# Linear attention and a leaky-ReLU layer pair on one core: tile 6's second layer as seven block products, the last batch's attention earlier

## The chip, the core and the metric

One core of a Trainium2 chip runs the whole kernel in one launch. The metric is device time in microseconds (us), lower is better. Beside the time of a run stands the span of a profiled execution: from its first to its last instruction.

## What is computed

Eight batches, eight heads, 576 rows and 64 columns a head give 4608 tokens of 512 features. `q` is made a softmax over its columns, `k` a softmax over the rows; the attention is linear (no product of q with k). Its output goes through two layers:

```python
kv = np.einsum('bhsd,bhse->bhde', k_s, v)            # per head 64 x 64
x  = np.einsum('bhsd,bhde->bhse', q_s, kv)           # then (4608, 512)
h  = x @ w_in                                        # (4608, 2048)
g  = np.maximum(0.01 * h, h)
out = g @ w_out                                      # (4608, 512)
```

## The kernel before, in words

The 4608 tokens are nine tiles of 512 (tiles 0 to 8). TensorE does all products: the attention of each batch, then for each tile the first layer (16 blocks of hidden features, line 563) and the second (line 584, 64 matmuls of 512 columns for a tile). The attention is spread over the tiles: softmax of batch b + 1, its `kv` and the attention of batch b run while tile t's layers are on TensorE. The order on every engine is written out by hand. `at(t, u, ...)` (line 595) puts functions at a place: in tile t, u from 0 to 15 is behind that block of the first layer, u from 16 to 31 is behind a quarter of a 128-token part of the second layer. All engines take their instructions in this program order, and each waits in its own queue for what it reads; VectorE (DVE), ScalarE (ACT) and GpSimd (POOL) do the elementwise work, SyncE (SP) issues most DMAs, among them a transposing DMA per batch (`q_turn`, line 548) which brings the softmax of q into the layout that the attention reads.

The hand-written places that the change touches (lines 740 to 776): `k_front` takes the maximum of k over rows (`k_tree`, `k_allmax`) and subtracts it, `q_front` does the same for q, `q_exp` and `k_exp` are ACT's exponentials, `q_back` sums, normalizes and issues the transposing DMA, `casts` turns v to bf16 on POOL, `attend_kv(b)` does the attention of batch b mixed with the `kv` product of batch b + 1. The last batch, 7, has its attention behind tile 6's first layer (line 850).

Tiles 7 and 8 are computed differently, since both come last and all their operands are in SBUF. Their two layers use a 2 x 2 block scheme in which seven products take the place of eight (Strassen's, in Winograd's form). For the first layer the blocks are the two tiles' tokens (`XA`, `XB`) against the two halves of features and hidden units: for each of the eight pairs of hidden blocks, `pair_layer1(i, fills)` (line 1046, called a round here, i = 0 to 7) makes seven products of two matmuls. Some of the operands are sums of blocks: `s1` to `s4` of tokens (`token_sums`, line 832), `t1` to `t4` of weights (`in_weight_sums`, line 812, POOL), copied to a type that fp32r matmuls take. In a round, `px` is one PSUM bank to which four products are added one after the other, and it is copied out between them (`e1`, `u2`, `u3`): `pair_first` makes the first one, `t2`·`s2`, `t3`·`s3` and `t4`·`a22` follow, each of them waiting for the copy before it. `pw` (`pair_second`) and `py` (`t1`·`s1`, and later `b22`·`s4` in `pair_third`) are banks of their own. The results are summed on DVE (line 1018), go through `leaky` (line 572, ACT's Prelu) and are kept in bf16 as rows `g7` and `g8`.

While a round waits for its copies, TensorE is given other work, the *fill*: the second layer of tile 6. `fill_steps` yields after each matmul, and `between(n)` takes n of them; the tuple in line 1101 says how many go into which of a round's three places. The first quarter of tile 6's second layer, with the first products of round 0, runs ahead of the rounds (line 1097).

For the second layer of tiles 7 and 8 (from line 1107) each tile is its own 2 x 2 scheme: tokens and hidden units are halved, and the output columns `E1`, `E2`. The weights' sums `v1` to `v4` and a copy `o22` are made once (`out_weight_sums`, line 804); the row sums `r1` to `r4` and the copy `c22` for each tile. Each product is 16 matmuls of 256 columns (line 1118). Tile 7's `r1` and `r3` begin on POOL during the rounds (`sums_ahead`, line 999).

Of the kernel before, what the change touches and what calls it, by code (L numbers as in the profile page):

```python
# [20 lines left out]
L = 64  # L21
# [5 lines left out]
def kernel(  # L27
# [736 lines left out]
    at(2, 27, lambda: attend_kv(3))  # L764
    for t in range(3, B - 1):
        b, last = t + 1, t + 2 == B
        q_front(b, t - 1, 19 if last else 29)
        at(t - last, 24 if last else 2, lambda b=b: q_exp(b, ALLR))
        if not last:
            k_front(b + 1, t, 1, 8)  # L770
            casts(b + 1, t, 6)
            at(t, 17, lambda b=b: k_exp(b + 1, ALLH))
            at(t, 23, lambda b=b: attend_kv(b))
        q_back(b, t - last, 25 if last else 5)
        if b + 2 < B:
            at(t, 5, lambda b=b: load_all(b + 2))

# [25 lines left out]

    def out_weight_sums():
        w = lambda fh, os: w_out_sb[:, fh * NH : (fh + 1) * NH, os]
        subtract(nc.vector, "v1", w(0, E2), w(0, E1))
        subtract(nc.vector, "v2", w(1, E2), plain("v1"))
        subtract(nc.vector, "v3", w(1, E2), w(0, E2))
        subtract(nc.vector, "v4", w(1, E1), plain("v2"))
        nc.gpsimd.tensor_copy(out=late["o22"], in_=w(1, E2))  # L810

    def in_weight_sums(i):
        w = lambda cs, fh: w_in_sb[:, cs, (fh * NH + i) * P : (fh * NH + i + 1) * P]
        for n, k in zip(("t1", "t2", "t3", "t4"), range(4)):
            late[n, i] = late["t"][:, k, i % 2 * 256 : i % 2 * 256 + 256].rearrange("p (c f) -> p c f", c=2)
        for n, x, y in (
            ("t1", w(CL, 1), w(CL, 0)),
            ("t2", w(CR, 1), plain(("t1", i))),
            ("t3", w(CR, 1), w(CL, 1)),
            ("t4", w(CR, 0), plain(("t2", i))),  # L820
        ):
            subtract(nc.gpsimd, (n, i), x, y)
        if i > 1:
            last_weights(i)

    def last_weights(i):
        late["b22", i] = late["pool"].tile([P, 2, P], F32R, name="b22")
        nc.gpsimd.tensor_copy(out=late["b22", i], in_=w_in_sb[:, CR, (NH + i) * P : (NH + i + 1) * P])

    pairs = ctx.enter_context(ExitStack())  # L830

    def token_sums():
# [10 lines left out]
        subtract(nc.vector, "s4", xT[:, CR, XA], plain("s2"))  # L843
        last_weights(0)
        last_weights(1)
# [93 lines left out]
    def layer2_at(t, g, tsub, pool=psO_pool, tag="pout"):  # L939
        po = pool.tile([P, O], FP32, name="pout", tag=tag)  # L940
        for j in range(NF):
# [5 lines left out]
            yield  # L947

    for t in range(1, TA):
        g_sb = []  # L950
        for j in range(NF):
            ph = psB_pool.tile([P, TT], FP32, name="ph", tag=BANK_TAG)
            layer1(j, ph, t * TT, TT)
            if j % 2 == 0:
                g_sb.append(g_pool.tile([P, 2, TT], BF16, name="gj"))
            leaky(g_sb[j // 2][:, j % 2], ph)
# [41 lines left out]

    def sums_ahead(n, names=("r1", "r3")):
        if n == 0:  # L1000
            for name in ("r3", "r1"):
                late_rows(name, name, late["ahead"])
        (ms, h0), (_, h1) = g7_blocks(0)[n], g7_blocks(1)[n]
        ops = dict(r1=(h1(0), h1(1), ALU.add), r3=(h0(0), h1(0), ALU.subtract))
        for name in names:
            x, y, op = ops[name]
            eng = nc.vector if n == 3 else nc.gpsimd
            eng.tensor_tensor(out=late[name][:, ms], in0=x, in1=y, op=op)

    def bank():  # L1010
        return psB_pool.tile([P, TT], FP32, name="pp", tag=BANK_TAG)

    def product(ps, w, a, first=True):
        for c in range(2):
            nc.tensor.matmul(ps, lhsT=w(c), rhs=a(c), start=(first and c == 0), stop=(c == 1), skip_group_check=True)  # L1015

    def add(o, ps, e):
        nc.vector.tensor_tensor(out=o, in0=ps, in1=e, op=ALU.add)  # L1018

    of = lambda n: (lambda c: late[n][:, c])  # L1020
    keep = lambda n: late["pool"].tile([P, TT], FP32, name=n)
    firsts, thirds = {}, {}

    def pair_first(i):
        ps, e1 = bank(), keep("e1")
        product(ps, lambda c: w_in_sb[:, c, i * P : (i + 1) * P], lambda c: xT[:, c, XA])
        nc.scalar.copy(out=e1, in_=ps)
        firsts[i] = ps, e1

# [4 lines left out]

    def pair_c11(i, ps):
        e1 = firsts[i][1]
        add(e1, ps, e1)
        leaky(g7[i], e1)

    def pair_third(i):  # L1040
        py, u2 = thirds[i]
        product(py, of(("b22", i)), of("s4"), False)
        add(u2, py, u2)
        leaky(g7[NH + i], u2)

    def pair_layer1(i, fills):
        px = firsts[i][0]
        u2, u3 = keep("u2"), keep("u3")
        g7_rows(i)
        if i == 0:  # L1050
            pw = pair_second(i)
            between(2)
        product(px, of(("t2", i)), of("s2"), False)
        if i:
            nc.vector.tensor_copy(out=u2, in_=px)
            pw = pair_second(i)
        else:
            nc.scalar.copy(out=u2, in_=px)
        if i + 1 < NH:
            pair_first(i + 1)  # L1060
        if i:
            pair_c11(i, pw)
            pair_third(i - 1)
        between(fills[0])
        product(px, of(("t3", i)), of("s3"), False)
        if i:
            nc.vector.tensor_copy(out=u3, in_=px)
        else:
            nc.scalar.copy(out=u3, in_=px)
            pair_c11(i, pw)  # L1070
        py = bank()
# [3 lines left out]
        add(u3, py, u3)  # L1075
        leaky(g8(NH + i), u3)
        if i == 0:
            nc.gpsimd.tensor_copy(out=gate, in_=u3[:, 0:1])
# [3 lines left out]
        if i + 2 < NH:  # L1082
            in_weight_sums(i + 2)
        if i in (2, 4, 6):
            sums_ahead(i // 2 - 1)

    def fill_steps():
        for tsub in range(1, NTS):
            yield from layer2_at(TA - 1, g_sb, tsub)

# [12 lines left out]
    next(fill, None)  # L1103
    pairs.close()
# [22 lines left out]
    def row_sums(wide, name, n, pool, op, x, y, eng=nc.vector):  # L1127
        late_rows(name, n, pool)
        for (ms, h0), (_, h1) in zip(wide(0), wide(1)):
            view = lambda s: late[s][:, ms].bitcast(FP32) if isinstance(s, str) else (h0, h1)[s[0]](s[1])  # L1130
            o = late[name][:, ms]
            if op is None:
# [11 lines left out]
    B8 = dict(t=TB, g=g8, wide=g8_wide, each=True, issue=(nc.sync, nc.scalar), r1="r1b", r2="r2b")  # L1144

    def put(z, o, half, i, cols, issues=None):
        for n, issue in enumerate(issues or z["issue"]):
            b, c = divmod(z["t"] * TT + half * M2 + i * P + n * L, S)
            issue.dma_start(out=out_r[b, c // L, :, cols], in_=o[n * L : (n + 1) * L, cols])

# [29 lines left out]
    def seventh(z):  # L1180
        product2(z["x"], rows("r3"), rows("v3"), z["each"], first=False)
        snap(z, "u3")

    def fourth(z):
        product2(z["x"], rows("c22"), rows("v4"), z["each"], first=False)
        for i in range(2):
            nc.scalar.copy(out=z["o2"][i][:, E1], in_=z["x"][i])
            put(z, z["o2"][i], 1, i, slice(0, O))

# [3 lines left out]
    def c11(z):  # L1193
        for i in range(2):
            add(z["o1"][i][:, E1], z["w"][i], z["e1"][:, i])
            put(z, z["o1"][i], 0, i, E1, (nc.sync, nc.sync))

# [4 lines left out]
    def c12(z):  # L1202
        for i in range(2):
            add(z["o1"][i][:, E2], z["y"][i], z["u2"][:, i])
            put(z, z["o1"][i], 0, i, E2)

    def sums(z, n):
        pool = late["ahead"] if n == "r3" else last_pool
        name = "r2b" if z is B8 and n == "r2" else n
        row_sums(z["wide"], name, name, pool, *dict(  # L1210
            r2=(ALU.subtract, z["r1"], (0, 0)),
# [11 lines left out]
    first(A)  # L1223
    sums_ahead(3, ("r1",))
    sums(A, "r2")
# [4 lines left out]
    c11(A)  # L1230
    sums_ahead(3, ("r3",))
    second(B8)
# [5 lines left out]
    seventh(A)  # L1238
    A["o2"], B8["o2"] = out_pairs(), [last_pool.tile([P, O], FP32, name=f"o{i}") for i in range(2)]
    sixth(B8)  # L1240
# [44 lines left out]
```

## Time and profile before

| | |
|---|---|
| median of 3 runs | 278.25 us (278.16 to 278.36) |
| the profiled execution | 278.23 us, of which the span is 276.4 us |
| instructions in the span | 5216, of these 2018 matmuls |
| TensorE clock granted | 1.00 throughout |
| HBM | 36.70 MB read, 9.44 MB written, 167 GB/s over the span |

All times within the execution are us from the span's start. A row of the chain or of a timeline begins with start and duration; matmuls overlap each other, so the pace is taken from start to start. A row of a group gives count, busy time and mean duration in ns of one, then the idle time of the engine before them and what ended it. PEld is TensorE's loading of weights. In the table of stages each engine has its busy us in the stretch and its count of instructions, then come the granted clock, the DMA share and GB/s.

### The profile page before, as it was taken

What the parts mean: (1) busy time and instruction counts of PE and PEld (TensorE: products, weight loads), DVE (VectorE), ACT (ScalarE), POOL (GpSimd) and SP (SyncE); (2) the same over time, 40 slices, a digit from 0 to 9 for tenths busy, and PEclk for the clock granted to TensorE, in tenths of its full rate; (3) what the DMA queues carried; (4) which work ended last, traced back from release to release, by engine and by line L of the source; (5) the groups of instructions that cost most, each with busy time, mean ns of one, the idle gap of its engine ahead of it and who ended that gap; (6) DMA issues with size and microseconds to landing.
All of it is one profiled execution on the core that took longest, in us unless ns stands there. A gap on an engine that the chain in (4) does not pass through costs nothing.

```text
span 276.4 us, 5216 instructions
## 1 busy us (share of the span) xinstructions
PE 269.2 (97%) x2018; PEld 148.8 (54%) x2018; DVE 215.0 (78%) x301; ACT 171.1 (62%) x304; POOL 81.9 (30%) x103
## 2 busy tenths in 40 slices
PE   7799999999999999999999999999999999999994
PEld 3378644444444454445444544454444656669994
DVE  2995995999999939975976397976958686769961
ACT  3977573784489366855486539665676676664241
POOL 2866460149003003100400076002000879910000
PEclk9999999999999999999999999999999999999999
DMA  7999999987996598079608950420611010101254
GB/s 241 333 209 322 242 267 259 392 284 231 252 391 244 92 364 299 2 166 393 195 0 178 384 170 22 85 57 21 133 30 40 0 38 13 28 11 40 66 115 115
DMA packets 40568, 46.48 MB, mean 168 GB/s; under 512 B 18912, under 2 KB 24288, under 8 KB 40544
## 3 DMA queue, kind: packets, MB, share of 16 engines
q1 hardware_dynamic: 36720, 41.56, 49.9%
q0 software_dynamic: 3504, 4.20, 8.7%
q10 hardware_dynamic: 320, 0.39, 0.4%
q8 instruction: 16, 0.26, 0.4%
q14 instruction: 8, 0.07, 0.1%
HBM read 36.70 MB, written 9.44 MB: 167 GB/s over the span
## 4 chain that ended last, share of the span: by engine, by line
PE 93%; DVE 3%; DMA 2%; ACT 0%; issue 0%; SPq 0%
PE pout L584 35%; PE ph L563 35%; PE pq L1118 9%; PE pp L1015 9%; DMA k_raw<-in_k_dram 2%; PE po L479 2%; DVE t L160 1%; PE pokv L341 1%; PE pkv L341 1%; PE pkv L419 0%; DVE k_raw L410 0%; ACT ke L206 0%; DVE kmax L160 0%; DVE kd L434 0%; PE pokv L479 0%
## 5 line engine op out<-in xcount | busy, mean ns | idle before, releaser
L584 PE MATMUL pout<-w_out_sb,gj 128*128 128x512 bf16 x448 | 101.6, 379 | 0.0
L563 PE MATMUL ph<-xT,w_in_sb 128*128 128x512 bf16 (+1 forms) x512 | 98.7, 352 | 0.0
L572 ACT ACTIVATE gj<-ph 128x512 bf16<-128x512 f32 x112 | 63.5, 602 | 19.0 <-PE ph L563 18.5
L563 PEld LDWEIGHTS <-w_in_sb 128*128 128x128 bf16 x512 | 49.8, 98 | 47.0 <-issue 0.2
L584 PEld LDWEIGHTS <-gj 128*128 128x128 bf16 x448 | 42.4, 98 | 51.7 <-issue 2.9
L218 POOL CAST vb<-v_raw 128x1152 bf16<-128x1152 f32 x13 | 19.3, 1510 | 82.3 <-DMA v_raw<-in_v_dram 82.0
L578 ACT COPY out_sb<-pout 128x512 f32<-128x512 f32 x24 | 14.0, 584 | 34.7 <-PE pout L584 20.7
L321 DVE TENSOR_REDUCE qsum<-qe 128x36 f32<-128x2304 bf16 (+5 forms) x13 | 20.1, 1543 | 6.5 <-ACT qe L312 6.4
L206 ACT ACTIVATE ke<-k_raw 128x2304 bf16<-128x2304 f32 (+2 forms) x13 | 18.0, 1383 | 7.9 <-DVE k_raw L198 7.4
L328 DVE TENSOR_TENSOR qe<-qe,qrec 128x2304 bf16<-128x2304 bf16 (+5 forms) x13 | 21.5, 1656 | 0.4
L245 DVE TENSOR_REDUCE qmax<-q_raw 128x36 f32<-128x2304 f32 (+5 forms) x13 | 20.0, 1537 | 0.4 <-DMA q_raw<-in_q_dram 0.4
L312 ACT ACTIVATE qe<-q_raw 128x2304 bf16<-128x2304 f32 (+5 forms) x13 | 17.2, 1322 | 4.2 <-POOL q_raw L304 3.2
L198 DVE TENSOR_TENSOR k_raw<-k_raw,kall 128x1152 f32<-128x1152 f32 (+2 forms) x10 | 18.0, 1821 | 0.3
L304 POOL TENSOR_TENSOR q_raw<-q_raw,qmax 128x512 f32<-128x512 f32 (+3 forms) x7 | 11.8, 1680 | 20.7 <-DVE qmax L245 19.2
L361 DVE RECIPROCAL krec<-pokv 128x2 f32<-128x2 f32 x8 | 1.3, 165 | 16.8 <-PE pokv L479 16.8
L1015 PE MATMUL pp<-s,t 128*128 128x512 f32 x48 | 14.1, 403 | 0.0
L500 ACT CAST xT<-po 128x448 bf16<-128x448 f32 (+3 forms) x31 | 13.3, 515 | 1.1 <-PE po L479 1.1
L160 DVE TENSOR_TENSOR t<-t 128x256 f32<-128x256 f32 (+2 forms) x22 | 13.1, 593 | 0.7
L304 DVE TENSOR_TENSOR q_raw<-q_raw,qmax 128x2304 f32<-128x2304 f32 (+1 forms) x6 | 13.4, 2232 | 0.2
L160 DVE TENSOR_TENSOR t<-k_raw 128x512 f32<-128x512 f32 (+1 forms) x11 | 12.1, 1102 | 1.2 <-DMA k_raw<-in_k_dram 1.1
L1018 DVE TENSOR_TENSOR u<-pp,u 128x512 f32<-128x512 f32 x16 | 11.1, 691 | 2.5 <-PE pp L1015 0.9
L791 POOL TENSOR_TENSOR t<-w_in_sb 128x256 fp32r<-128x256 bf16 x16 | 11.9, 745 | 0.5 <-PE pp L1015 0.5
(134 smaller groups left out, 324.4 us busy)
## 6 DMA issues: line engine op xcount, KB each, us to landing
out_dram<-out_sb SPq DMA_DIRECT2D x60, 128.0 KB, 4.1
k_raw<-in_k_dram SPq DMA_DIRECT2D x8, 576.0 KB, 5.9
v_raw<-in_v_dram SPq DMA_DIRECT2D x8, 576.0 KB, 9.0
q_raw<-in_q_dram SPq DMA_DIRECT2D x4, 1152.0 KB, 9.1
v_raw<-in_v_dram SPq DMA_DIRECT2D x4, 1152.0 KB, 11.5
k_raw<-in_k_dram SPq DMA_DIRECT2D x4, 1152.0 KB, 6.9
q_raw<-in_q_dram SPq DMA_DIRECT2D x4, 576.0 KB, 7.7
w_in_sb<-in_moe_w_in_dram POOLq DMA_DIRECT2D x7, 256.0 KB, 6.8
```

Source lines behind the costliest of these rows:

```text
L160: nc.vector.tensor_tensor(out=o, in0=i0, in1=i1, op=ALU.max)
L198: eng.tensor_tensor(out=ks, in0=ks, in1=st[b]["kall"][:, hs].unsqueeze(2).to_broadcast([P, n, R, D]), op=ALU.subtract,)
L218: eng.tensor_copy(out=o, in_=i)
L245: nc.vector.tensor_reduce(out=o, in_=st[b]["q"][:, hs, rs], axis=AX.X, op=ALU.max)
L304: eng.tensor_tensor(out=qs, in0=qs, in1=st[b]["qmax", rs.start, hs.start].unsqueeze(3).to_broadcast([P, m, n, D]), op=ALU.subtract,)
L321: nc.vector.reduce_sum(out=qsum, in_=q_cols(b, rs, hs), axis=AX.X)
L328: nc.vector.tensor_tensor(out=qes if out is None else out, in0=qes, in1=st[b]["qrec", rs.start, hs.start].unsqueeze(3).to_broadcast([P, n, ...
L563: nc.tensor.matmul(ph, lhsT=w_in_sb[:, cb, j * P : (j + 1) * P], rhs=xT[:, cb, c0 : c0 + n], start=(cb == 0 and first), stop=(cb == NB - 1 ...
L572: nc.scalar.activation(out=o, in_=ph, func=AF.Prelu, alpha=LEAKY_SLOPE)
L584: nc.tensor.matmul(pout, lhsT=g_sb[j // 2][:, j % 2, tsub * P : (tsub + 1) * P], rhs=w_out_sb[:, j, os], start=(j == 0), stop=(j == NF - 1),)
L1015: nc.tensor.matmul(ps, lhsT=w(c), rhs=a(c), start=(first and c == 0), stop=(c == 1), skip_group_check=True)
L1118: nc.tensor.matmul(ps[i], lhsT=a(m)[:, i * P : (i + 1) * P], rhs=w(m), start=(first and m == 0 and (each or i == 0)), stop=(m == NH - 1 an ...
```

## The change

1. Tile 6's second layer gets the 2 x 2 scheme too. `fill_steps` is rewritten: seven products of 16 matmuls with 256 columns, 112 in all instead of 64 with 512 columns. Two products (on `g` as it is) are bf16, five read fp32r sums. They use two PSUM banks of the `pout` kind, in three tiles (`pw`, `py`, `px`).
2. Tile 6's row sums: `r1`, `r2` on DVE (`six_first`, four blocks, three of them during tile 6's first layer), `r3` and `r4` on POOL at the end of rounds 1, 2 and 3, and the copy `c22` on ACT in round 5. Three SBUF places (`alpha`, `beta`, `r3lo`) are shared by tile 6's sums and then tile 7's.
3. Evictions of the fill: ACT copies of 256 columns instead of 512, and DVE additions in rounds 3, 5 and 7; two stores at the end of round 7 each.
4. The quarter of tile 6's second layer ahead of the rounds is gone; `pair_first(0)` goes between the last two blocks of tile 6's first layer, and the numbers of fill steps are new.
5. In a round: `b22` is cast by ACT instead of POOL; `u2` is always copied by DVE; `u3` by ACT in rounds 0, 3, 5 and 7; the Prelus of `g7` move behind that copy. One more of tile 7's `r3` blocks is summed by DVE in the last stage, and tile 7's `r1` and `r3` on POOL come later (rounds 5 and 6).
6. The last batch's attention moves from behind tile 6's first layer to tile 5's second layer, at (5, 29), with the token sums. For that, batch 6's q front, batch 7's k front and q work, and their exponentials and transposing DMAs move ahead by up to one tile. `v1` and `o22` are made at (5, 26), `v2` to `v4` at (6, 4).

The diff, cut to its core:

```diff
-    for t in range(3, B - 1):
...
+    for t in range(3, B - 3):
...
+    q_front(6, 4, 18)
+    at(4, 26, lambda: q_exp(6, ALLR))
+    k_front(7, 4, 29, 40)
+    q_back(6, 5, 1)
+    q_front(7, 5, 2)
+    casts(7, 5, 6)
+    at(5, 12, lambda: q_exp(7, ALLR))
+    q_back(7, 5, 16)
+    at(5, 17, lambda: k_exp(7, ALLH))
+    at(5, 23, lambda: attend_kv(6))
...
-        if i > 1:
-            last_weights(i)
...
-        nc.gpsimd.tensor_copy(out=late["b22", i], in_=w_in_sb[:, CR, (NH + i) * P : (NH + i + 1) * P])
+        nc.scalar.copy(out=late["b22", i], in_=w_in_sb[:, CR, (NH + i) * P : (NH + i + 1) * P])
...
-    at(6, 2, out_weight_sums)
+    at(5, 26, lambda: out_weight_sums("o22", "v1"))
-    at(6, 15, lambda: attend_all(B - 1, (R7, both), (RE, both, psO_pool, "pout")), token_sums)
+    at(5, 29, lambda: attend_all(B - 1, (R7, both), (RE, both)), token_sums)
+    at(6, 4, lambda: out_weight_sums("v2", "v3", "v4"))
...
+    def six_sums(n, k):
+        (ms, h0), (_, h1) = six_blocks(0)[k], six_blocks(1)[k]
+        part = lambda n: late[n][:, ms].bitcast(FP32)
+        if n == "c22":
+            nc.scalar.copy(out=late["6c22"][:, ms], in_=h1(1))
+            return
+        x, y, op = dict(
+            r1=lambda: (h1(0), h1(1), ALU.add),
+            r2=lambda: (part("6r1"), h0(0), ALU.subtract),
+            r3=lambda: (h0(0), h1(0), ALU.subtract),
+            r4=lambda: (h0(1), part("6r2"), ALU.subtract),
+        )[n]()
+        eng = nc.vector if n in ("r1", "r2") else nc.gpsimd
+        eng.tensor_tensor(out=late["6r2" if n == "r4" else "6" + n][:, ms], in0=x, in1=y, op=op)
...
+    for n in range(3):
+        at(6, 10 + 2 * n, lambda n=n: six_first(n))
+    at(6, 14, lambda: pair_first(0))
...
     def pair_layer1(i, fills):
-        px = firsts[i][0]
+        px, e1 = firsts[i]
...
         if i == 0:
             pw = pair_second(i)
-            between(2)
+            between(8)
         product(px, of(("t2", i)), of("s2"), False)
+        nc.vector.tensor_copy(out=u2, in_=px)
...
+        last_weights(i)
+        early.pop(i, lambda: None)()
+        add(e1, pw, e1)
         if i:
-            pair_c11(i, pw)
             pair_third(i - 1)
+        else:
+            six_first(3)
         between(fills[0])
         product(px, of(("t3", i)), of("s3"), False)
+        if i in (0, 3, 5, 7):
+            nc.scalar.copy(out=u3, in_=px)
+        else:
+            nc.vector.tensor_copy(out=u3, in_=px)
+        leaky(g7[i], e1)
...
+        for n in {1: (0, 1), 2: (2, 3)}.get(i, ()):
+            six_sums("r3", n)
+        for n in {3: range(4)}.get(i, ()):
+            six_sums("r4", n)
...
     def fill_steps():
-        for tsub in range(1, NTS):
-            yield from layer2_at(TA - 1, g_sb, tsub)
...
+        yield from steps(pw, lambda m: g(NH + m)[:, 0:M2], w_first(1))
...
+        yield from steps(py, rows("6r1"), rows("v1"))
...
+        yield from steps(px, lambda m: g(m)[:, 0:M2], w_first(0))
...
+        yield from steps(px, rows("6r2"), rows("v2"), False)
...
+        yield from steps(px, rows("6r3"), rows("v3"), False)
...
+        yield from steps(py, rows("6r2"), rows("o22"), False)
...
+        yield from steps(px, rows("6c22"), rows("v4"), False)
...
-    for n, _ in enumerate(layer2_at(TA - 1, g_sb, 0, psB_pool, BANK_TAG)):
-        if n == 9:
-            pair_first(0)
     for i in range(NH):
-        pair_layer1(i, ((3, 3, 0), *[(0, 6, 0)] * 4, *[(0, 5, 0)] * 2, (1, 4, 1))[i])
+        pair_layer1(i, ((6, 6, 0), (0, 12, 0), *[(0, 16, 0)] * 4, (0, 6, 0), (2, 6, 2))[i])
```

More of the change, by code (lines that the diff above doesn't have):

```diff
@@ L764 @@
     at(2, 27, lambda: attend_kv(3))
-    for t in range(3, B - 1):
[L766 to L776, printed above, removed]
+    for t in range(3, B - 3):
+        b = t + 1
+        q_front(b, t - 1, 29)
+        at(t, 2, lambda b=b: q_exp(b, ALLR))
+        k_front(b + 1, t, 1, 8)
+        casts(b + 1, t, 6)
+        at(t, 17, lambda b=b: k_exp(b + 1, ALLH))
+        at(t, 23, lambda b=b: attend_kv(b))
+        q_back(b, t, 5)
+        at(t, 5, lambda b=b: load_all(b + 2))
+    q_front(6, 4, 18)
[8 more added lines that the diff above has]
+    at(5, 23, lambda: attend_kv(6))
     TA, TB = NT - 2, NT - 1
@@ L947, in layer2_at, with bank, product, add @@
             yield
+    def bank():
+        return psB_pool.tile([P, TT], FP32, name="pp", tag=BANK_TAG)
+    def product(ps, w, a, first=True):
+        for c in range(2):
+            nc.tensor.matmul(ps, lhsT=w(c), rhs=a(c), start=(first and c == 0), stop=(c == 1), skip_group_check=True)
+    def add(o, ps, e):
+        nc.vector.tensor_tensor(out=o, in0=ps, in1=e, op=ALU.add)
+    of = lambda n: (lambda c: late[n][:, c])
+    keep = lambda n: late["pool"].tile([P, TT], FP32, name=n)
+    firsts, thirds = {}, {}
+    def pair_first(i):
+        ps, e1 = bank(), keep("e1")
+        product(ps, lambda c: w_in_sb[:, c, i * P : (i + 1) * P], lambda c: xT[:, c, XA])
+        nc.scalar.copy(out=e1, in_=ps)
+        firsts[i] = ps, e1
     for t in range(1, TA):
@@ L997, in late_rows, with r3_rows, sums_ahead @@
         late[name] = pool.tile([P, NH, M2], F32R, name=n)
[L999 to L1002, printed above, removed]
+    def r3_rows(ms):
+        return late["r3lo"] if ms.start < NH // 2 else late["r3"]
+    def sums_ahead(n, names=("r1",)):
+        if n == 0 and "r1" in names:
+            home("r1", "beta")
+            late["r3lo"] = late["ahead"].tile([P, NH // 2, M2], F32R, name="r3lo")
+        if n == 2 and "r3" in names:
+            home("r3", "alpha")
         (ms, h0), (_, h1) = g7_blocks(0)[n], g7_blocks(1)[n]
@@ L1006, in sums_ahead @@
             x, y, op = ops[name]
[L1007 to L1028, printed above, removed]
+            eng = nc.vector if n > (2 if name == "r1" else 1) else nc.gpsimd
+            o = (late[name] if name == "r1" else r3_rows(ms))[:, ms]
+            eng.tensor_tensor(out=o, in0=x, in1=y, op=op)
     def pair_second(i):
@@ new lines, in pair_layer1, with pair_third, put @@
+        if i == NH - 2:
+            sums_ahead(2)
+            for n in range(2):
+                sums_ahead(n, ("r3",))
+    def pair_third(i):
+        py, u2 = thirds[i]
+        product(py, of(("b22", i)), of("s4"), False)
+        add(u2, py, u2)
+    early, late_in = {}, {}
+    def put(o, t, half, i, cols, issues=(nc.sync, nc.sync)):
+        for n, issue in enumerate(issues):
+            b, c = divmod(t * TT + half * M2 + i * P + n * L, S)
+            issue.dma_start(out=out_r[b, c // L, :, cols], in_=o[n * L : (n + 1) * L, cols])
@@ L1180, in seventh @@
     def seventh(z):
-        product2(z["x"], rows("r3"), rows("v3"), z["each"], first=False)
+        product2(z["x"], lambda m: r3_rows(slice(m, m))[:, m], rows("v3"), z["each"], first=False)
         snap(z, "u3")
@@ L1204, in c12 @@
             add(z["o1"][i][:, E2], z["y"][i], z["u2"][:, i])
[L1205 removed]
+            put(z["o1"][i], z["t"], 0, i, E2, z["issue"])
     def sums(z, n):
[L1208 removed]
         name = "r2b" if z is B8 and n == "r2" else n
[L1210 removed]
+        row_sums(z["wide"], name, name, last_pool, *dict(
             r2=(ALU.subtract, z["r1"], (0, 0)),
@@ L1230 @@
     c11(A)
-    sums_ahead(3, ("r3",))
+    for n in range(2, 4):
+        sums_ahead(n, ("r3",))
     second(B8)
@@ L1238 @@
     seventh(A)
-    A["o2"], B8["o2"] = out_pairs(), [last_pool.tile([P, O], FP32, name=f"o{i}") for i in range(2)]
+    A["o2"], B8["o2"] = out_pairs(), last_pairs()
     sixth(B8)
```

131 lines of the change are left out of this document (95 added, 36 removed).

## The prediction

> **What bounds the kernel now.** I read the busy shares and the chain first, then the table of stages, the chain row by row, and last the queues of the other engines.
>
> ```profile
> PE 269.2 (97%) x2018; PEld 148.8 (54%) x2018; DVE 215.0 (78%) x301; ACT 171.1 (62%) x304; POOL 81.9 (30%) x103
> PE 93%; DVE 3%; DMA 2%; ACT 0%; issue 0%; SPq 0%
> ```
>
> The end is set by TensorE: 97% busy, 93% of the chain. Only something that shortens TensorE's own work, or that makes it wait, moves the end. The table of stages (columns PE, PEld, DVE, ACT, POOL busy, clock) gives the first layer of tile 6, the joint first layer of tiles 7 and 8 with tile 6's second layer as fill, and their second layer:
>
> ```profile
> 192.39:206.20 13.81, 13.81 (x68) 6.15 (x70) 11.26 (x5) 9.47 (x16) 0.00 (x0) 1.00 0.40 81
> 206.20:246.60 40.40, 40.40 (x194) 23.33 (x195) 30.22 (x44) 27.74 (x49) 25.39 (x39) 1.00 0.09 20
> 246.60:276.40 29.80, 26.18 (x224) 25.27 (x222) 20.20 (x29) 10.54 (x21) 0.00 (x0) 1.00 0.34 81
> ```
>
> TensorE has no gap in the first two, at full clock. DVE has 10.2 us free in the second, ACT 12.7, POOL 15.0: that is the cover the change can spend. The chain in order of time shows what TensorE does in the second of these:
>
> ```profile
> 206.20 0.61 PE po L479 x16
> 206.81 2.26 PE pout L584 x10
> ...
> 218.03 1.31 PE pout L584 x6
> 219.34 3.19 PE pp L1015 x14
> ...
> 246.59 26.21 PE pq L1118 x224
> ```
>
> The last batch's attention (po) is 0.61; a round is 14 products of the joint layer in 3.19 and six matmuls of tile 6's second layer in 1.31, which is 0.218 each. The 64 of them cost 64 x 0.218 = 13.97.
>
> **The change, part by part.** *The products.* 64 matmuls of 512 columns go; seven block products of 16 matmuls with 256 columns come, 112 in all. Two of them (pw, c11) are bf16, five take fp32r sums. The last stage has both kinds already:
>
> ```profile
> 246.88 3.22 PE L1118 MATMUL pq<-w_out_sb,xT 128*128 128x256 bf16 x28
> 249.94 0.60 PE L1118 MATMUL pq<-w_out_sb,gj 128*128 128x256 bf16 x4
> ...
> 259.18 2.08 PE L1118 MATMUL pq<-v,r2b 128*128 128x256 f32 x16
> 261.10 2.08 PE L1118 MATMUL pq<-v,c 128*128 128x256 f32 x16
> ```
>
> From start to start, 28 bf16 ones take 249.94 - 246.88 = 3.06, 0.109 each; 16 fp32r ones take 261.10 - 259.18 = 1.92, 0.120 each. So the fill costs 32 x 0.109 + 80 x 0.120 = 3.50 + 9.60 = 13.10: **0.87 us less**. An eighth of the multiplications is gone, but half of that goes back to the slower fp32r matmuls. Why they are slower can be seen in their weight loads:
>
> ```profile
> L1118 PEld LDWEIGHTS <-xT 128*128 128x128 bf16 x56 | 5.5, 98 | 0.6
> L1118 PEld LDWEIGHTS pq<-v,r2b 128*128 128x128 f32 x16 | 2.0, 192 | 0.0
> ```
>
> A load of 98 ns fits beside a matmul of 109; one of 192 doesn't. The Trainium skill (TensorE: Matmul & The Clock Gate, Back-to-back issue gap) gives an isolated gap of N / 2.4 GHz + 2.5 ns, 109 ns for 256 columns whatever the type; by it the fill would take 112 x 0.109 = 12.2 and the gain be 1.8. The bf16 rows agree with it and the fp32r rows don't, so I go by the rows.
>
> *The attention.* Its 0.61 moves from 206.20 to tile 5's second layer, eight matmuls before its end: nothing lost or won on TensorE, if batch 7 is ready. What must be ready is a chain on DVE. Rows of its steps as they run before:
>
> ```profile
> 156.50 0.17 DVE L361 RECIPROCAL krec<-pokv 128x2 f32<-128x2 f32 x1 [6.36 <-PE pokv L479]
> 157.31 2.54 DVE L245 TENSOR_REDUCE qmax<-q_raw 128x36 f32<-128x2304 f32 x1
> 162.55 2.16 DVE L160 TENSOR_TENSOR t<-k_raw 128x1024 f32<-128x1024 f32 x1
> 166.64 0.78 DVE L160 TENSOR_TENSOR kmax<-t,k_raw 128x256 f32<-128x256 f32 x1
> 168.73 2.55 DVE L321 TENSOR_REDUCE qsum<-qe 128x36 f32<-128x2304 bf16 x1 [1.31 <-ACT qe L312]
> 174.21 0.44 DVE L167 STREAM_TRANSPOSE kmaxT<-kmax 128x256 f32<-128x256 f32 x1
> 178.98 2.55 DVE L245 TENSOR_REDUCE qmax<-q_raw 128x36 f32<-128x2304 f32 x1
> 185.42 0.17 DVE L361 RECIPROCAL krec<-pokv 128x2 f32<-128x2 f32 x1 [1.30 <-PE pokv L479]
> ```
>
> A q front takes 162.55 - 157.31 = 5.2, a q back 174.21 - 168.73 = 5.5, the rest of a k front 178.98 - 174.21 = 4.8, a k tree 166.64 + 0.78 - 162.55 = 4.9. Batch 6's q front now falls into the 6.36 that DVE was idle before 156.50. From 157.3 on DVE then runs k tree 7, q back 6, q front 7, k max and subtraction 7, q back 7: 4.9 + 5.5 + 5.2 + 4.8 + 5.5 = 25.9, to 183.2, before the krec at 185.42. ACT reaches the moved q exponential after its thirteenth Prelu of tile 5, near 175.4 (a Prelu comes every 13.81 / 16 = 0.86), when the q subtraction (172.9) is done. It holds ACT for 2.12, which is less than three of TensorE's six banks. SP then issues the DMA transpose:
>
> ```profile
> 166.58 2.12 ACT L312 ACTIVATE qe<-q_raw 128x2304 bf16<-128x2304 f32 x1
> 194.89 2.68 SPq L551 DMA_TRANSPOSE qX<-qe  x1
> DMA to landing us min/median/max: 4.6/4.6/4.6
> ```
>
> 183.2 + 4.6 = 187.8. TensorE asks for it 24 matmuls after the preceding attention, whose end starts the krec at 185.4: 185.4 + 24 x 0.218 = 190.6: **2.8 us to spare**. On SP it stands ahead of tile 5's four stores, which wait some 3 us more; their buffers aren't asked for until the fill's first copies, 20 us on.
>
> *DVE ahead of the rounds.* Copies of the attention, token sums, three remaining weight sums and six row sums of tile 6:
>
> ```profile
> 201.46 2.29 DVE L791 TENSOR_TENSOR v<-w_out_sb,v 128x2048 fp32r<-128x2048 bf16 x1
> 206.59 1.49 DVE L502 CAST xT<-po 128x448 bf16<-128x448 f32 x3 [2.85 <-PE po L479]
> 208.17 1.23 DVE L839 TENSOR_TENSOR s<-xT 128x1024 fp32r<-128x1024 bf16 x1
> 212.84 0.68 DVE L1018 TENSOR_TENSOR e<-pp,e 128x512 f32<-128x512 f32 x1
> 248.62 0.69 DVE L1135 TENSOR_TENSOR r<-r,gj 128x512 fp32r<-128x512 f32 x1
> ```
>
> From 191.0: 1.5 + 4.7 (208.17 to 212.84) + 3 x 2.27 + 6 x 0.61 = 16.7, to 207.7. The joint layer's first copy on DVE comes near 209.0. Covered, 1.3 to spare.
>
> *The rounds.* TensorE needs 3.19 + 16 x 0.120 = 5.11 in the full rounds, and 4.6 in round 1. DVE has five operations of 0.69 (four where ACT takes a copy) and at most two of 0.42 more: under 4.3. ACT, by these groups:
>
> ```profile
> L1027 ACT COPY e<-pp 128x512 f32<-128x512 f32 x8 | 4.7, 587 | 4.1 <-PE pp L1015 4.1
> L572 ACT ACTIVATE xT<-u 128x512 bf16<-128x512 f32 x14 | 8.8, 631 | 4.3 <-DVE u L1018 4.2
> L1155 ACT COPY gu<-pq 128x256 f32<-128x256 f32 x6 | 2.1, 374 | 2.9 <-PE pq L1118 2.9
> L1133 ACT CAST c<-gj 128x512 fp32r<-128x512 bf16 x1 | 0.6, 634 | 0.0
> ```
>
> The cast of b22 by ACT isn't shown: between nothing beyond the 0.37 of a copy of that size and the 0.63 of a cast of twice it; I take 0.4. A round has 0.59 + 0.4 + 3 x 0.63 + 0.59 (a Prelu from PSUM, taken like the copy) = 3.5, 0.59 more where ACT takes the copy, 0.75 more where a block product is evicted: at most 4.8 of 5.11. **Round 5** has the four casts besides: 4.1 + 4 x 0.63 = 6.6 against 5.11, then rounds 6 and 7 with 3.5 and 4.8 against 3.9 and 4.5. Behind the casts stand round 5's last Prelu and round 6's copy of e1; TensorE asks for that e1 only in round 7, and the bank that the Prelu frees is asked for two rounds on. By my rows the copy of round 7 that TensorE does wait for ends half a us before it is asked for. Cost nothing; if the cover fails, up to the backlog of some 1.1.
>
> *POOL.* It loses eight casts of b22 and wins eight sums:
>
> ```profile
> 163.60 1.64 POOL L791 TENSOR_TENSOR t<-w_in_sb 128x256 fp32r<-128x256 bf16 x1
> 226.53 2.28 POOL L1008 TENSOR_TENSOR r<-gj 128x512 fp32r<-128x512 bf16 x2
> L791 POOL TENSOR_TENSOR t<-w_in_sb,t 128x256 fp32r<-128x256 bf16 x12 | 8.1, 678 | 0.5
> ```
>
> From round 0's end near 212.3 to the last r4: four sets of weight sums, 16 x 0.68 = 10.9, and eight sums of 1.14 = 9.1: to 232.3. Round 5's fill reads r4 near 234.8. 2.5 to spare. The Trainium skill (SBUF — State Buffer, on the port pair that VectorE and GpSimd share) has a GpSimd read blocked by a VectorE instruction with two SBUF inputs. The first row above (1.64 instead of 0.68, beside a DVE maximum of two SBUF tiles) agrees. In these rounds DVE reads PSUM and one SBUF tile, and there the sums ran at 1.14.
>
> *The last stage.*
>
> ```profile
> 265.14 0.76 DVE L1018 TENSOR_TENSOR out_sb<-pq,gu 128x256 f32<-128x256 f32 x2 [2.12 <-PE pq L1118]
> ```
>
> DVE has one sum of 0.61 more there, and its first sum waits for the last Prelu, some 0.6 later behind TensorE than now by the sums above. Ahead of this row it idles for 2.12, after tile 8's r3 sums, the ones with the least to spare: 2.12 - 1.2 = 0.9 is left. Nothing.
>
> **The sum**, against the profiled execution (278.23, span 276.4; the median of the runs is 278.25): 278.23 - 0.87 = 277.36. The first ten matmuls of tile 6's second layer took 2.26, 0.08 more than ten of 0.218, and that spot goes too: **277.3**.
>
> **The rivals.** *ACT bounds the last rounds* (20%): the backlog of 1.1 out of round 5 lands on TensorE, through round 7's copy or through the Prelus that the last stage's first products read. For it: 6.6 against 5.11 in one round. Against: the slack worked out above. 277.3 + 1.1 = 278.4, no change. *POOL is late with r4* (9%), the one that ends slower: if the eight sums and the weight sums run against DVE's port, TensorE stands in round 5 and all behind it. It decides from 2.5 us in 20.0, a slow-down of 1.13; at 1.25 r4 comes at 237.3, 2.5 late: 279.8. The first four POOL rows at 163.60 were slowed more than that, those at 226.53 not at all. *Batch 7's attention is late* (7%): past its 2.8 us to spare each us falls on TensorE in full; 4 us late gives 278.5, 6 us 280.5. *All fill matmuls go at the bf16 rows' 0.109* (5%): 13.97 - 112 x 0.109 = 1.8 is gained, 276.4. *The fill doesn't run at the rows' pace between matmuls of 512 columns* (5%): at 0.125 each it costs 14.0, and the gain is gone: 278.2.
>
> **How the numbers follow.** The forecast has 54%, with 277.1 to 277.6 as its own spread. A measurement of this kernel tells 0.2% (0.56 us, 277.69) from no change. Faster: 54 + 5, and a little of the ACT case, 0.60. Same: most of the ACT case, the slow fill and a part of the late attention, 0.24. Slower: 0.16. The range goes from 276.7 to 278.8: forecast, ACT case and slow fill, leaving out the full pace and the two late cases, some 2 in 10.
>
> **What would show it.** Right: the stage from tile 6's first layer to the last product shorter by 0.9 with TensorE still without gaps; 112 fill matmuls at 0.109 and 0.120. Wrong: a wait of TensorE at the moved attention, in round 5's fill (POOL), in rounds 6 and 7 (ACT), or a fill matmul above 0.12.

## The result: 0.3% faster, from the fill

The changed kernel takes 277.47 us, the median of ten runs (277.24 to 278.08), against 278.31 us (278.16 to 278.76) for the kernel before on the same chip. The ratio is 0.9969, with an interval from 0.9959 to 0.9979. The forecast was 277.3. The profiled execution took 277.72 us, its span is 275.8 us and the clock 1.00.

Busy shares and shares of the chain of the changed kernel (engine, busy us, share, instructions):

```profile
PE 268.4 (97%) x2041; PEld 156.3 (57%) x2066; DVE 220.8 (80%) x314; ACT 175.8 (64%) x322; POOL 89.9 (33%) x102
PE 93%; DVE 3%; DMA 2%; issue 1%; ACT 0%; SPq 0%
```

TensorE is still the bound. It has 48 matmuls more, as the counts of weight loads (PEld) tell, 2066 against 2018. Of its 2066 matmuls this profile has 2041, so the busy times of PE can't be compared to a tenth; the starts in the chain can. Each of the three elementwise engines has got more to do. Table of stages of the changed kernel (tile 6's first layer, the rounds, the last stage; columns as in the prediction):

```profile
193.00:207.20 14.20, 14.10 (x65) 6.42 (x66) 14.10 (x12) 10.52 (x18) 0.00 (x0) 1.00 0.09 19
207.20:246.00 38.80, 38.59 (x222) 29.84 (x225) 26.74 (x45) 29.68 (x62) 30.52 (x38) 1.00 0.00 1
246.00:275.80 29.80, 26.16 (x224) 25.24 (x222) 20.71 (x30) 10.61 (x22) 0.00 (x0) 1.00 0.46 107
```

The middle stage was 40.40 and is 38.80; 0.61 of the 1.60 less is the attention, which has left it. TensorE still waits for nothing in it: the 0.21 us that its busy time leaves open stand where three records of matmuls are missing (222 against 225 loads). DVE now works through the whole of the first stage, where it had 2.5 us free. The chain in order of time says where the time came from (start, us, engine, tile, line, matmuls); first the changed kernel:

```profile
185.64 0.32 PE pout L584
...
190.92 0.61 PE po L479 x16
191.54 1.83 PE pout L584 x8
...
206.32 0.43 PE pp L998 x2
...
207.61 0.43 PE pp L998 x2
208.05 0.87 PE pout L1165 x8
...
216.75 3.20 PE pp L998 x14
219.95 1.76 PE pout L1165 x16
...
230.03 1.92 PE pout L1165 x16
...
245.97 26.20 PE pq L1252 x224
```

and one row of the kernel before, the end of the last joint attention and `kv` product:

```profile
185.37 7.01 PE pout L584 x32
```

From that end to the last stage it was 246.59 - 185.37 = 61.22 and is 245.97 - 185.64 = 60.33: 0.89 less. The last stage is as long as before (26.20 and 26.21). The span keeps only 0.6 of it, since this execution came to that end 0.27 later; in the profiles of those variants below whose program is the same up to there, the end lies anywhere from 185.2 to 185.7. The twelve `pout` pieces of line 1165 add up to 13.07 us for 112 matmuls, where 13.10 was forecast: 16 bf16 ones in 1.76, 16 fp32r ones in 1.92.

### The profile page after: what moved, and what is told of

Same layout as the page of the kernel before. It is cut to its first block, busy times and chain, and to the rows that moved or that the text cites. A ratio compares the mean times of both kernels' runs of the same rounds, so it can differ in the third digit from the quotient of the medians.

```text
span 275.8 us, 5326 instructions
## 1 busy us (share of the span) xinstructions
PE 268.4 (97%) x2041; PEld 156.3 (57%) x2066; DVE 220.8 (80%) x314; ACT 175.8 (64%) x322; POOL 89.9 (33%) x102
## 4 chain that ended last, share of the span: by engine, by line
PE 93%; DVE 3%; DMA 2%; issue 1%; ACT 0%; SPq 0%
PE ph L563 35%; PE pout L584 30%; PE pq L1252 9%; PE pp L998 9%; PE pout L1165 5%; DMA k_raw<-in_k_dram 2%; PE po L479 2%; DVE t L160 1%; PE pokv L341 1%; PE pkv L341 1%; PE pkv L419 0%; DVE k_raw L410 0%; ACT ke L206 0%; DVE kmax L160 0%; DVE kd L434 0%
## 5 line engine op out<-in xcount | busy, mean ns | idle before, releaser
L584 PE MATMUL pout<-w_out_sb,gj 128*128 128x512 bf16 x371 | 84.6, 379 | 0.9 <-issue 0.3
L584 PEld LDWEIGHTS <-gj 128*128 128x128 bf16 x384 | 36.7, 98 | 43.6 <-issue 0.2
L578 ACT COPY out_sb<-pout 128x512 f32<-128x512 f32 x20 | 11.7, 584 | 30.3 <-PE pout L584 19.1
L198 DVE TENSOR_TENSOR k_raw<-k_raw,kall 128x1152 f32<-128x1152 f32 (+2 forms) x10 | 18.7, 1885 | 0.3
L799 POOL TENSOR_TENSOR t<-w_in_sb 128x256 fp32r<-128x256 bf16 x16 | 15.5, 971 | 0.0
L1095 DVE COPY u<-pp 128x512 f32<-128x512 f32 x8 | 5.5, 691 | 10.9 <-PE pp L998 10.9
L160 DVE TENSOR_TENSOR t<-k_raw 128x512 f32<-128x512 f32 (+1 forms) x11 | 11.2, 1015 | 1.3 <-DMA k_raw<-in_k_dram 1.2
```

Source lines behind the costliest of these rows:

```text
L160: nc.vector.tensor_tensor(out=o, in0=i0, in1=i1, op=ALU.max)
L198: eng.tensor_tensor(out=ks, in0=ks, in1=st[b]["kall"][:, hs].unsqueeze(2).to_broadcast([P, n, R, D]), op=ALU.subtract,)
L584: nc.tensor.matmul(pout, lhsT=g_sb[j // 2][:, j % 2, tsub * P : (tsub + 1) * P], rhs=w_out_sb[:, j, os], start=(j == 0), stop=(j == NF - 1),)
```

## The experiments

In each, the ratio is against the kernel before on the same chip (medians there 278.24 to 278.32).

**1. Which of the two parts gains?** `move_alone` is the kernel before with the last batch's attention, its softmax and the token sums moved as in the change, and the old fill:

```diff
-    at(6, 15, lambda: attend_all(B - 1, (R7, both), (RE, both, psO_pool, "pout")), token_sums)
+    at(5, 29, lambda: attend_all(B - 1, (R7, both), (RE, both)), token_sums)
```

> The kernel before with one part of the change alone: the last batch's attention and token sums at tile 5's second layer, with the softmax schedule that goes with it; tile 6's second layer stays as it was. Theory (the gain is the cheaper fill, the move is worth nothing on TensorE by itself): 278.2 to 278.4 us, no change against before. Rival (the move brings the gain, since a wait around the attention goes): 277.4 to 277.6 us, as the whole change.

278.38 us, ratio 1.0001 [0.9992, 1.0010]. The move alone changes nothing that can be measured: TensorE does the same matmuls at another place. `fill_alone` is the changed kernel with the attention back behind tile 6's first layer, and so with the token sums and the first row sums behind it:

```diff
-    at(5, 29, lambda: attend_all(B - 1, (R7, both), (RE, both)), token_sums)
...
-    for n in range(3):
-        at(6, 10 + 2 * n, lambda n=n: six_first(n))
-    at(6, 14, lambda: pair_first(0))
+    at(6, 15, lambda: attend_all(B - 1, (R7, both), (RE, both)), token_sums)
+    at(6, 15, lambda: pair_first(0), *[lambda n=n: six_first(n) for n in range(3)])
```

> The changed kernel with the attention, its softmax schedule and the token sums put back behind tile 6's first layer; the block products stay, and the three early row sums of tile 6 stand behind the token sums. Theory (the move pays for the cover of the sums on VectorE): x_keep copies 1.5, token sums 4.7 and six row sums 3.7 from 206.6 on stand ahead of round 0's u2 copy, which ends near 217.3 instead of 209.7; TensorE waits about 8 us: 285 us. Rival (the sums aren't on the path, the gain is TensorE's pace alone): 277.4 us.

287.76 us, ratio 1.034 [1.0322, 1.0359], 10.3 more than the whole change. So the move gains nothing, yet the new fill can't do without it. Two rows of TensorE's timeline and one of DVE's (start, us, operation, idle time before and what ended it), and a stretch of the table of stages:

```profile
210.69 0.70 PE L988 MATMUL pp<-s,t 128*128 128x512 f32 x2 [1.61 <-DVE s L791]
217.55 2.05 PE L988 MATMUL pp<-s,t 128*128 128x512 f32 x4 [5.05 <-DVE u L1085]
216.72 0.68 DVE L1085 COPY u<-pp 128x512 f32<-128x512 f32 x1
217.50:223.50 6.00, 5.95 (x17) 3.88 (x18) 3.17 (x5) 2.89 (x6) 2.76 (x5) 0.50 0.00 0
```

TensorE waits for a token sum, and then 5.05 for the first copy of `px`, which stands on DVE behind the token sums and six row sums. That makes 6.66 of the 10.3. After the long wait the granted clock is 0.50 for 6 us, in which it does the work of 3: together 9.7. My expectation had the waits and not the clock. The profiled execution (288.40, mean clock 0.986) is one of the two longer ones; the other two of the four took 287.12 and 287.25 at 0.994.

**2. Does the pace hang on the type?** `second_bf16` writes all sums of the second layers (`r`, `c`, `v`) as bf16 instead of fp32r, `both_bf16` those of the first layer too. The sums are rounded to bf16 by that, which the reference doesn't do.

```diff
-        late[n] = late["ahead"].tile([P, NH, M2], F32R, name=n, tag=buf)
+        late[n] = late["ahead"].tile([P, NH, M2], BF16, name=n, tag=buf)
```

(and the same for the other tiles of sums).

> The changed kernel with all block sums and weight sums of the second layers (tiles 6, 7, 8) kept in bf16 instead of fp32r, so their rounding is coarser than in the reference. Theory (pace by type, 0.120 against 0.109 a matmul of 256 columns): 80 fill matmuls and 160 of the last stage at 0.011 less each: 0.9 + 1.7, so 274.9 us. Rival (VectorE's sums bound the last stage as soon as TensorE is faster, 0.6 to 0.9 us to spare): some 1.5 us, 276 us.

275.58 us, ratio 0.990 [0.9887, 0.9914], 0.7 above the 274.9 expected.

> As the run with the second layer's sums in bf16, and the joint first layer's token sums, weight sums and copies in bf16 too. Theory (an fp32r matmul of 512 columns takes 0.233 against 0.2165 for bf16, worked out from a round's 5.12 us): 80 more matmuls at 0.017 less: 1.3 us below the other run, 273.5 us. Rival (with shorter rounds ScalarE and VectorE bound them): no less than the other run, 274.9 us.

273.94 us, ratio 0.9854 [0.9828, 0.9880], 1.64 below `second_bf16` where 1.3 was expected; its four runs lie from 273.40 to 275.60. Chain rows of `second_bf16`:

```profile
229.77 1.76 PE pout L1165 x16
...
236.49 3.41 PE pp L998 x14
...
245.63 24.48 PE pq L1252 x224
```

The last stage's 224 matmuls take 24.48 instead of 26.20, and a fill of 16 takes 1.76 instead of 1.92: 0.109 each, like those on unsummed rows. So the type sets the pace, in the fill as in the last stage. Not all of the fill's part arrived: from the fill's start to the last stage it was 245.97 - 208.05 = 37.92 in the changed kernel and is 245.63 - 208.08 = 37.55 here, 0.37 less instead of 0.9. The round from 236.49 has 3.41 for its 14 products instead of 3.20, and behind it up to the last stage nothing is gained (5.73 against 5.69), which experiment 6 follows up.

**3. Is the weight load the reason for the pace?** These rows of loads (line, operands, count, busy us, mean ns) are of the changed kernel, then of `second_bf16`:

```profile
L998 PEld LDWEIGHTS pp<-s,t 128*128 128x128 f32 x48 | 8.8, 188 | 1.9
L1165 PEld LDWEIGHTS pout<-v,6r 128*128 128x128 f32 x48 | 6.2, 189 | 0.2
```

```profile
L1252 PEld LDWEIGHTS <-r 128*128 128x128 bf16 x80 | 7.8, 98 | 0.9
```

and a chain row of `bf16_no_copies` (experiment 6), whose products of the joint layer are all bf16:

```profile
235.12 3.02 PE pp L997 x14
```

There 14 products take 3.02, 0.216 each. In the changed kernel ten of the 14 are fp32r and they take 3.20: the ten are (3.20 - 4 x 0.216) / 10 = 0.234 each. Their load of 188 ns is shorter than either, so it would fit beside the matmul, and they are still 8% slower. At 256 columns, a load of 189 ns doesn't make the pace 0.189 but 0.120: the 48 loads of line 1165 are busy for 6.2 in all, less than 48 x 0.189 = 9.1, so they overlap each other. The prediction's reason, that a load longer than the matmul holds it up, doesn't hold at 512 columns, and at 256 it doesn't give the pace. What sets it is open: no run here pairs weights of one type with tokens of the other.

**4. How much do POOL and ACT have to spare?** `pool_2_more` and `pool_4_more` give POOL two and four further sums ahead of `r4` (into a place that is written again before it is read), `casts_twice` makes ACT cast `c22` twice in round 5.

```diff
+            for n in range(4):
+                (_, h0), (_, h1) = six_blocks(0)[n], six_blocks(1)[n]
+                nc.gpsimd.tensor_tensor(out=late["r3lo"][:, 0:2], in0=h0(0), in1=h1(0), op=ALU.subtract)
+            for n in range(4):
+                six_sums("r4", n)
```

> The changed kernel with two more sums of the size of r3 on GpSimd ahead of the four r4 sums in round 3 (into a place that is used only later). Theory (r4 has some 2 us to spare before round 5's fill): 2.3 us later, the last r4 lands near 235.0, its reader stands near 235.7: no change, 277.4 us. Rival (GpSimd already sets round 5): plus 2.3 us, 279.8 us.

277.36 us, ratio 0.9969 [0.9957, 0.9981].

> As the run with two more sums on GpSimd ahead of r4, with four. Theory: 4.6 us later, the last r4 lands near 237.3 where its reader would stand at 235.7: TensorE waits 1.6 us in round 5: 279.0 us. Rival (GpSimd's sums are covered wherever they stand): 277.4 us.

279.36 us, ratio 1.0051 [1.0033, 1.0069]. The last `r4` sums on POOL and the fill that reads them, in the changed kernel:

```profile
228.08 4.58 POOL L883 TENSOR_TENSOR 6r<-gj,6r 128x512 fp32r<-128x512 bf16 x4
234.99 2.08 PE L1165 MATMUL pout<-o,6r 128*128 128x256 f32 x16
```

and in `pool_4_more`:

```profile
232.53 4.55 POOL L883 TENSOR_TENSOR 6r<-gj,6r 128x512 fp32r<-128x512 bf16 x4
236.02 0.51 PE L1169 MATMUL pout<-o,6r 128*128 128x256 f32 x2 [0.62 <-POOL 6r L883]
237.14 1.45 PE L1169 MATMUL pout<-o,6r 128*128 128x256 f32 x10 [0.62 <-POOL 6r L883]
```

`r4` is ready at 228.08 + 4.58 = 232.66 and the fill that reads it begins at 234.99: 2.33 to spare (2.5 forecast, from 232.3 to 234.8). The last of the four sums has more, since that fill takes the blocks in order and comes to the last two with its seventh matmul, at 234.99 + 6 x 0.120 = 235.7: 3.0. Two sums of 4.58 / 4 = 1.15 leave some 0.7 of that and cost nothing; four make it 237.08, and TensorE waits twice.

> The changed kernel with round 5's four casts (c22 of tile 6) made twice by ScalarE. Theory (ScalarE's backlog out of round 5 stays just under what rounds 6 and 7 can take): 2.1 us more moves round 6's copy of e1 to 242.0, 0.7 past where TensorE asks for it, and round 7's copy 0.2 later still: plus 0.9, 278.3 us. Rival (ScalarE is far from the path): 277.4 us.

278.73 us, ratio 1.0016 [1.0007, 1.0026]: 1.26 more than the change for four casts, which take 4.15 / 2 = 2.1. The chain of `casts_twice` shows how ACT's backlog arrives:

```profile
236.53 4.15 ACT 6c L874 x8
...
241.18 0.47 ACT e L1010
```

and the rows of the two waits, TensorE's and DVE's:

```profile
241.79 0.70 PE L998 MATMUL pp<-s,t 128*128 128x512 f32 x2 [0.61 <-ACT e L1010]
243.88 1.17 PE L998 MATMUL pp<-s,t 128*128 128x512 f32 x4 [0.24 <-DVE u L1095]
243.04 0.69 DVE L1095 COPY u<-pp 128x512 f32<-128x512 f32 x1 [1.92 <-ACT xT L572]
```

The first wait is the copy of `e1` that the prediction named. The second isn't in it: DVE's copy `u2` had to wait 1.92 for a place that an older Prelu on ACT was still reading. So ACT's queue reaches TensorE through DVE as well. In the changed kernel neither wait is there.

**5. How much has the attention to spare, and what do DVE's sums cost?** `attention_8_earlier` puts the attention at (5, 27), eight matmuls ahead of its place, `attention_earlier` at (5, 24), four matmuls behind the preceding one; nothing else changes.

```diff
-    at(5, 29, lambda: attend_all(B - 1, (R7, both), (RE, both)), token_sums)
+    at(5, 27, lambda: attend_all(B - 1, (R7, both), (RE, both)), token_sums)
```

> The changed kernel with the last batch's attention eight matmuls earlier, at (5, 27). Theory (with tile 5's stores beside it the transposing DMA lands 6.2 us after its issue at 183.4, at 189.6): TensorE asks near 189.1 and waits 0.5 us, too short to lower its clock: 277.9 us. Rival (it lands after 4.6 us, as in the kernel before, at 188.0): no wait, 277.4 us. A third outcome: a short wait lowers the clock too, 279 us or more.

278.23 us, ratio 0.9997 [0.9987, 1.0007].

> The changed kernel with the last batch's attention 20 matmuls earlier, at (5, 24). Theory (the transposed softmax lands near 187.9, 3.0 us before it is asked for at (5, 29)): TensorE asks at 186.4 and waits 1.4 us: 278.8 us. Rival (the transposing DMA is long done, the place is free): 277.4 us.

281.13 us, ratio 1.0091 [1.0056, 1.0126]; its runs lie from 279.11 to 283.45, and the profiled one is among the longer (span 280.8). First a row of `attention_8_earlier`, then of `attention_earlier` the attention, the DMA that it waits for and three stretches of the table of stages:

```profile
189.69 0.68 PE L479 MATMUL po<-qX,kd 64*64 64x448 bf16 x16 [0.72 <-ACT out_sb L578]
```

```profile
189.61 1.15 PE L479 MATMUL po<-qX,kd 64*64 64x448 bf16 x16 [3.13 <-DMA qX<-qe]
183.26 6.21 DMA qX<-qe
189.60:191.00 1.40, 1.39 (x17) 0.79 (x18) 0.75 (x2) 0.80 (x2) 0.00 (x0) 0.53 0.22 50
191.00:193.00 2.00, 2.00 (x6) 0.76 (x5) 1.90 (x3) 1.49 (x3) 0.00 (x0) 0.50 0.00 0
193.00:195.00 2.00, 2.00 (x11) 0.88 (x9) 1.97 (x3) 0.34 (x1) 0.00 (x0) 0.98 0.00 0
```

Batch 7 is there at about 189.6 in both (in the first, the profile names a copy of ACT's that ended as the DMA landed, so which of the two came last isn't told). The wait of 0.72 costs 0.8 and no more; the wait of 3.13 is followed by 3.4 us at half clock, which costs another 1.7. My expectation had 278.8 and a wait of 1.4: the DMA of 6.2 and the clock were left out. But not every run has both. Four took 279.11 to 279.39 with a mean clock of 1.00, near the expectation; two took 280.95 and 281.30, also at 1.00; the other four took 282.35 to 283.45, at 0.994 and 0.986. That would fit a DMA of 4.6 in the first four and of 6.2 in the rest, with a halved clock only in the last four; one execution was profiled, so it isn't shown.

`sums_on_dve` gives `r3` and `r4` to DVE instead of POOL:

```diff
-        eng = nc.vector if n in ("r1", "r2") else nc.gpsimd
+        eng = nc.vector
```

> The changed kernel with tile 6's r3 and r4 on VectorE instead of GpSimd, at the same places in the program. Theory (GpSimd's share of the sums keeps VectorE free for the copies that the rounds wait for): the r3 pairs at the end of rounds 1 and 2 take 1.3 us each and end before the next u2 copy is due; the four r4 at the end of round 3 take 2.5 us from 226.9 on and end at 229.3, so round 4's u2 copy ends at 230.0 where its reader stands at 228.9: plus 1.1, 278.6 us. Rival (the placing is worth nothing, VectorE has 9 us free in the stage): 277.4 us.

279.72 us, ratio 1.0052 [1.0037, 1.0067], 2.3 more than the change instead of 1.1. Its rows on DVE and POOL, and the longer of the two waits of TensorE (1.7 together); below, DVE's sums of the same shape in the changed kernel:

```profile
226.26 3.59 DVE L883 TENSOR_TENSOR 6r<-gj,6r 128x512 fp32r<-128x512 bf16 x4
226.50 1.12 POOL L799 TENSOR_TENSOR t<-w_in_sb 128x256 fp32r<-128x256 bf16 x1
231.85 0.68 POOL L799 TENSOR_TENSOR t<-w_in_sb 128x256 fp32r<-128x256 bf16 x1 [3.15 <-PE pp L998]
230.60 1.17 PE L998 MATMUL pp<-s,t 128*128 128x512 f32 x4 [1.39 <-DVE u L1095]
```

```profile
L883 DVE TENSOR_TENSOR 6r<-gj 128x512 fp32r<-128x512 bf16 x4 | 2.7, 683 | 0.0
```

A sum of two SBUF tiles takes DVE 0.683 while POOL does nothing. The four here take 0.955 each on average and 3.59 in a row, where 2.5 was expected. The POOL sums that run beside them take 1.12 instead of 0.68. The Trainium skill (SBUF — State Buffer, Who interferes with whom) says that a DVE instruction with two SBUF inputs contends with a GpSimd one that reads SBUF; these rows agree. In the changed kernel DVE has no sum of two SBUF tiles while `r4` is made, and POOL's `r4` ran at 1.15, near the 1.14 that the prediction took.

**6. A version that gains more.** With all sums in bf16, operands that were copied only for their type need no copy. `bf16_no_copies` is `both_bf16` without the copies `a22`, `b22`, `o22` and those of `c22`, for tile 6 and for tiles 7 and 8; the rounding is the same.

```diff
-        product(py, of(("b22", i)), of("s4"), False)
+        product(py, lambda c: w_in_sb[:, 2 + c, (NH + i) * P : (NH + i + 1) * P], of("s4"), False)
```

> As the run with both layers' sums in bf16, with the copies left out that were there only for the type: the casts of b22, a22, o22 and c22 go, and the products read weights, tokens and hidden rows as they are. Theory (what both_bf16 lost against its pace in rounds 6 and 7, 0.3 us or so, is ScalarE's backlog out of round 5): 273.6 us. Rival (it is VectorE's u2 copy or GpSimd, which stay): 273.9 us.

273.38 us, ratio 0.9824 [0.9809, 0.9839], the fastest here. Its median is 0.56 below `both_bf16`, but the intervals of the two overlap, so the traces have to tell. Chain rows of `both_bf16`, then of `bf16_no_copies`:

```profile
235.24 1.31 PE pp L998 x6
...
243.81 24.47 PE pq L1252 x224
```

```profile
243.36 24.47 PE pq L1250 x224
```

From the start of the round to the last stage it was 243.81 - 235.24 = 8.57 and is 243.36 - 235.12 = 8.24: 0.33 less, the 0.3 of the expectation. The row at 235.12 above is the round that took 3.41 in `second_bf16`; here it takes 3.02, like the rounds ahead of it. DVE's copies are still there, and of what was left out only `o22` isn't ACT's work and is made long before. So the loss comes from ACT's queue; that the smaller one of `second_bf16` does too fits, but wasn't tried by itself. Like `both_bf16` this version trades the precision of the sums for its time.

## Why the prediction was right, step by step

*The products (0.87 less): right.* The pieces sum to 13.07 against 13.10, and what they replace to 14.05 in the chain before against 13.97. From the end of tile 6's first layer to the last stage it was 246.59 - 206.81 = 39.78. Now that end is at 207.61, and 0.43 of `pair_first` runs ahead of it (206.32), so it is 245.97 - 207.61 + 0.43 = 38.79: 0.99 less, of which 0.87 + 0.08 had been forecast. The 0.08 is won there and lost again where the attention now stands, as the next point but one shows. The rivals "bf16 pace" and "slow fill" are out by the rows of 1.92.

*Its reason (the load of 192 ns): not borne out.* The price came from rows and was right; the mechanism given for it fails on the 512-column matmuls (experiment 3). That the price came out was not the mechanism's doing: the rows of the last stage had the same types and widths as the new fill.

*The attention (nothing on TensorE): right, with a spare that was mis-sized.* `move_alone` is the direct test. Its chain behind the moved attention, and at the attention's old place:

```profile
191.52 1.83 PE pout L584 x8
...
207.17 2.16 PE pout L584 x10
```

The ten matmuls at the old place take 2.16 instead of 2.26, and the eight behind the attention take 1.83, 0.229 each, where eight of 0.218 take 1.74. So the 0.08 that the sum took off for "that spot" is real, but it moved with the attention: that term should have been nothing, and the forecast 277.4. This is why the changed kernel gains 0.89 from the end of the joint attention on, and not 0.99.

DVE's chain was forecast to end at 183.2 and the DMA was issued at 183.40, but it took 6.2 instead of 4.6. The group of the seven transposing DMAs, landing times as lowest, median and highest, before and after:

```profile
DMA to landing us min/median/max: 3.7/4.6/6.3
```

```profile
DMA to landing us min/median/max: 3.7/5.8/6.2
```

The prediction took one row's 4.6 where the group reached 6.3. The spare was 190.92 - 189.60 = 1.3 and not 2.8, so this rival was nearer than its 7% said. Why the same DMA takes 4.6 or 6.2 is open; the stores issued right behind it are not the reason by themselves, since stores stood right behind the one of 4.6 before (197.67) as well.

*DVE ahead of the rounds (1.3 to spare): right,* and the true worth of the move. Two rows of the changed kernel, the last of the six row sums and the first copy:

```profile
207.56 0.69 DVE L883 TENSOR_TENSOR 6r<-6r,gj 128x512 fp32r<-128x512 f32 x1
209.43 0.69 DVE L1095 COPY u<-pp 128x512 f32<-128x512 f32 x1 [1.18 <-PE pp L998]
```

The sums end at 208.25 (207.7 forecast), and DVE idles for 1.18 ahead of the copy. The prediction priced this step only as cover. `fill_alone` shows the price when it fails: 10.3.

*The rounds and ACT (nothing): right, and near the edge.* A cast of `b22` takes 0.41 (0.4 taken), the four casts of `c22` 2.17 (2.5 taken). Four more of them cost 1.26, so the rival's mechanism is real and its size of the order given (1.1), but with four casts it doesn't come into play.

```profile
L840 ACT CAST b<-w_in_sb 128x256 fp32r<-128x256 bf16 x8 | 3.3, 409 | 0.0
236.79 2.17 ACT L874 CAST 6c<-gj 128x512 fp32r<-128x512 bf16 x4
```

*POOL (2.5 to spare): right.* 2.33 measured up to the fill's first matmul. The prediction took all four sums as needed there; the last one is needed six matmuls later, which leaves 3.0. Two further sums are free and four cost 1.9. The rival's mechanism, two engines on one port, exists, but where DVE does the sums (experiment 5).

*The last stage (0.9 to spare, nothing): right, with more to spare.* DVE idles 1.61 ahead of the same sum:

```profile
264.52 0.76 DVE L1001 TENSOR_TENSOR out_sb<-pq,gu 128x256 f32<-128x256 f32 x2 [1.61 <-PE pq L1252]
```

## What to carry to other kernels

An eighth fewer multiplications was worth only 7% of the fill (0.98 of 14.05), since sums kept in fp32r make each of its matmuls 10% slower: price a block scheme by the matmuls' rows of the type that they will have, and look at the copies that only change a type. A move that gains nothing by itself can be what makes another change possible: ask which engine's queue it empties ahead of the next stage, and what the stage would wait for without it. And take a spare time against the longest of a group of equal transfers, not against the nearest one.

## What the runs showed of the hardware beside that

- TensorE's granted clock halved after the two longest waits in mid-kernel that were profiled: after 3.13 us it was 0.50 to 0.53 for 3.4 us, after 5.05 us 0.50 for 6 us. After 0.72 us (`attention_8_earlier`), 1.39 (`sums_on_dve`) and 1.61 (`fill_alone`) it stayed at 1.00. The Trainium skill (TensorE: Matmul & The Clock Gate, Part 1: The HAM clock gate) has the rate halve after an idle window of about 3.4 us; the wait of 3.13 is a little shorter than that, the others agree, and where between 1.61 and 3.13 it begins no run here shows. In these two executions such a wait cost half as much again as its own length, or more.
- A matmul on fp32r operands is slower at both widths, 0.120 against 0.109 for 256 columns and 0.234 against 0.216 for 512, with loads of 188 to 192 ns against 98.
- DVE and POOL slow each other when both add SBUF tiles: DVE from 0.68 to 0.96 on average, POOL from 0.68 to 1.12.
